# A new issue table for a hand-scheduled kernel: the last token tile computed last in two column halves, and new time constants for the search

## The chip, the cores and the metric

One core of a Trainium2 chip (core 0, the only one that the runs list). The metric is device time in microseconds (us) of one execution, several executions each. Engines are named as in the profile: PE is TensorE (PEld its weight loads), DVE is VectorE, ACT is ScalarE, POOL is GpSimd, SP is SyncE, whose queue SPq issues transfers. The mean granted clock of a run differs (0.989 to 1.000).

## The reference

Two branches read the same layer-normalised input and are added to it. Shapes: 2048 tokens, width 640, hidden width 1728, all bf16.

```python
x = A_q                                   # [1, 2048, 640]
xn = layernorm(x)
# branch A: shifted keys times values, a causal convolution of length 2048 per channel, gated
kv = shift_conv4(k, shift_k) * v
y  = irfft(rfft(pad(kv)) * rfft(pad(ssm_k)))[:2048] + kv * ssm_D
# branch B: gated feed-forward
h  = sigmoid(xn @ w_gate) * (xn @ w_up)   # [2048, 1728]
return x + xn * y + h @ w_down
```

## The kernel before

The sum of all 2048 tokens stays on the chip, and almost everything is bf16. The feed-forward part runs in 4 groups of 512 tokens: 14 hidden chunks of up to 128, each a gate and an up product in PSUM (a "dense group": 5 matmuls of 512 columns), a sigmoid on ACT, a multiply into `hT` on DVE; then for each of the four 128-token tiles of a group a down projection in two column halves of 320. The convolution runs as a four-step Fourier transform in 10 blocks of channels (c1: into `T`, c2: into `S`, products on DVE, c3: into `V`, c4: into `xq`), each step a PE group into one of two PSUM buffers "c", evicted by ACT or DVE.

The instruction stream is not left to a scheduler. All work is recorded as some 950 numbered operations, and two tables, found by an offline search with a cost model, fix the rest: `ORDER` is the order in which they are issued, `ON_DVE` lists those that could run on ACT or DVE and are to run on DVE. The order within each engine is the order in the table; buffers are handed out in that order, too.

```python
ORDER = [6, 0, 5, 1, 4, 2, 8, ...]                    # 948 numbers
ON_DVE = [45, 133, 135, 620, ..., 553, 559]           # 40 numbers

    def table(self):
        dve = set(ON_DVE)
        for i in ORDER:
            o = self.ops[i]
            o.on = next(iter(o.engs)) if len(o.engs) == 1 else "DVE" if i in dve else "ACT"
        return [self.ops[i] for i in ORDER]

    SLOTS = {..., "T": 2, "S": 2, "P2": 1, "V": 1, "c": 2, "g": 4}   # buffers by kind; c and g are PSUM

    def ev(n, out_fn, in_fn, scale=None, **kw):       # an eviction: either engine may do it
        ...
        plan.op({"ACT": ((0.833 * n + 55) * 1e-3, fa), "DVE": ((1.042 * n + 75) * 1e-3, fd)}, **kw)

    def rec_rsq(m0, m1, pri):                         # inverse root of the variances: 13 small DVE instructions
        def rsq():
            nc.vector.tensor_scalar(ve, var, 1.0 / DM, 1e-5, op0=ALU.mult, op1=ALU.add)
            ...                                       # three Newton steps of three instructions
        dve(2400, 1, rsq, r=[("mv", m) for m in range(m0, m1)], ...)   # waits for ACT's sums of squares

    def rec_evac(tr, fc, cs, pri):                    # a pair of dense groups becomes one chunk of hT
        ...
        act(512, lambda: nc.scalar.activation(tl[sg][:], tl[cs[0]][:], ACT.Sigmoid), ...)
        dve(512, 1, lambda: nc.vector.tensor_tensor(hT[:, fc, :], tl[sg][:], tl[cs[1]][:], ALU.mult), ...)

    def rec_down(tr, out):
        for t4 in range(4):
            m = 4 * tr + t4
            last = m == NQ - 1
            parts = ([(0, 7, (0,)), (7, 14, (0,)), (0, 7, (1,)), (7, 14, (1,))] if last else
                     [(c0, c1, (0, 1)) for c0, c1 in ((0, 4), (4, 8), (8, 11), (11, 14))])
            ...
```

The costs in `ev` are constants of the search's model, not measurements: in the trace of the kernel before, an eviction of 1024 columns took 1.02 us on ACT and 1.22 on DVE.

Numbers that come up below: 132 the inverse root for tiles 8 to 15; 649/650 and 653/654 the first two dense pairs of token group 1; 652, 661, 706, 709 multiplies into `hT` for chunks 0, 2, 12, 13 of that group; 163, 164 shift multiplies of the convolution input of block 0; 714 the last part of the down projection of tile 4, which reads `hT` chunks 11 to 13; 227 to 233 second transforms of block 1; 694 a dense group; 180, 232, 258 evictions into `T`, `S`, `T`; 912 to 923 tiles 14 and 15.

Of the kernel before, what the change touches and what calls it, by code (L numbers as in the profile page):

```python
# [22 lines left out]
NQ = S // P  # L23
# [19 lines left out]
def _dft_tables():  # L43
# [37 lines left out]
    6, 0, 5, 1, 4, 2, 8, 7, 3, 11, 10, 13, 12, 9, 14, 16, 71, 72, 15, 73, 74, 75, 91, 17, 86, 76, 96, 77, 104, 97,  # L81
    78, 571, 81, 79, 87, 88, 82, 80, 83, 92, 89, 84, 90, 148, 85, 94, 93, 572, 98, 100, 99, 102, 101, 149, 103, 589,
    42, 150, 151, 152, 155, 153, 57, 154, 157, 563, 156, 158, 564, 64, 565, 590, 567, 566, 568, 569, 62, 573, 570,
    18, 61, 574, 575, 63, 577, 58, 576, 578, 579, 56, 581, 580, 582, 59, 583, 585, 107, 584, 106, 586, 607, 587, 108,
    591, 588, 66, 105, 592, 593, 608, 109, 110, 595, 594, 19, 111, 609, 596, 113, 43, 68, 597, 599, 60, 112, 598, 29,
    600, 601, 114, 603, 65, 604, 605, 602, 610, 67, 606, 611, 612, 39, 614, 613, 44, 615, 45, 133, 134, 20, 136, 616,
    617, 23, 619, 135, 618, 27, 620, 621, 116, 623, 31, 622, 625, 624, 118, 626, 115, 32, 627, 41, 120, 628, 119, 40,
    631, 122, 25, 629, 632, 121, 630, 35, 117, 633, 123, 634, 126, 637, 128, 635, 30, 636, 130, 638, 127, 639, 131,
    26, 640, 129, 37, 643, 642, 125, 641, 649, 124, 650, 132, 24, 651, 38, 653, 644, 655, 652, 21, 654, 162, 22, 69,
    645, 656, 646, 657, 658, 36, 647, 648, 33, 659, 660, 34, 163, 662, 95, 164, 165, 663, 664, 172, 167, 667, 665,  # L90
    137, 28, 661, 159, 666, 669, 166, 668, 161, 168, 47, 671, 160, 670, 50, 169, 672, 673, 48, 171, 143, 170, 46,
    178, 674, 144, 52, 173, 676, 180, 54, 179, 677, 138, 49, 174, 678, 51, 181, 175, 139, 680, 53, 675, 183, 182,
    290, 681, 682, 70, 176, 140, 195, 186, 685, 683, 141, 295, 196, 294, 199, 142, 177, 201, 200, 185, 686, 184, 202,
    145, 197, 293, 187, 689, 296, 198, 679, 291, 188, 687, 690, 292, 203, 297, 204, 192, 692, 189, 694, 205, 193,
    206, 695, 194, 207, 190, 209, 208, 191, 227, 210, 217, 228, 216, 233, 146, 234, 219, 211, 147, 218, 231, 220,
    212, 688, 232, 221, 229, 698, 298, 55, 230, 222, 684, 691, 223, 213, 696, 235, 699, 214, 249, 703, 236, 215, 237,
    701, 224, 238, 248, 704, 226, 240, 251, 225, 243, 239, 250, 259, 244, 697, 735, 260, 253, 265, 736, 693, 707,
    700, 252, 705, 266, 241, 755, 706, 711, 242, 702, 254, 261, 708, 263, 255, 262, 712, 280, 709, 264, 713, 267,
    245, 268, 717, 281, 246, 247, 714, 269, 718, 270, 283, 256, 715, 716, 719, 271, 257, 258, 723, 282, 272, 273,
    310, 274, 710, 720, 311, 275, 722, 721, 314, 276, 729, 315, 316, 299, 286, 312, 317, 730, 288, 313, 731, 318,  # L100
    277, 319, 287, 724, 278, 320, 732, 279, 321, 284, 322, 725, 285, 391, 734, 307, 301, 395, 300, 726, 309, 733,
    756, 737, 333, 308, 302, 324, 727, 739, 728, 394, 342, 323, 325, 738, 304, 397, 343, 303, 396, 344, 740, 346,
    392, 305, 345, 393, 332, 741, 347, 348, 743, 326, 349, 289, 742, 327, 350, 351, 746, 744, 374, 352, 367, 745,
    328, 748, 354, 747, 330, 329, 750, 353, 306, 388, 752, 775, 355, 751, 390, 331, 757, 749, 389, 334, 753, 358,
    336, 759, 356, 335, 359, 398, 754, 758, 337, 357, 338, 761, 760, 400, 368, 763, 401, 762, 399, 403, 369, 404,
    764, 766, 765, 371, 370, 767, 768, 372, 375, 769, 776, 770, 373, 381, 376, 772, 795, 771, 378, 797, 377, 777,
    773, 379, 339, 830, 779, 774, 380, 778, 341, 340, 360, 781, 402, 382, 783, 780, 782, 405, 406, 383, 784, 407,
    786, 384, 433, 385, 432, 411, 788, 785, 787, 435, 412, 386, 417, 436, 415, 418, 387, 790, 416, 413, 792, 789,
    791, 414, 796, 798, 419, 793, 420, 794, 361, 800, 362, 799, 363, 364, 365, 802, 801, 806, 803, 805, 422, 421,
    408, 424, 807, 423, 409, 434, 808, 410, 804, 425, 437, 366, 443, 426, 812, 438, 444, 439, 449, 465, 427, 450,  # L110
    464, 813, 467, 428, 468, 445, 447, 446, 809, 448, 814, 831, 810, 429, 811, 451, 815, 430, 431, 452, 818, 817,
    461, 816, 819, 462, 463, 820, 472, 821, 473, 466, 824, 474, 535, 542, 825, 469, 454, 440, 453, 826, 456, 442,
    827, 455, 441, 470, 459, 822, 457, 471, 460, 823, 549, 832, 829, 458, 556, 828, 475, 834, 499, 476, 833, 500,
    481, 835, 479, 482, 836, 480, 850, 503, 838, 477, 504, 837, 478, 505, 839, 483, 501, 484, 506, 840, 841, 502,
    842, 843, 493, 844, 845, 494, 495, 851, 846, 847, 486, 485, 496, 848, 488, 852, 487, 497, 498, 854, 491, 849,
    489, 492, 853, 490, 507, 508, 517, 855, 856, 518, 521, 858, 523, 522, 870, 857, 510, 871, 524, 509, 519, 859,
    512, 861, 520, 511, 860, 515, 863, 513, 516, 862, 514, 525, 526, 865, 864, 866, 867, 890, 891, 872, 868, 869,
    873, 527, 874, 528, 876, 529, 530, 877, 878, 875, 531, 879, 533, 880, 532, 881, 534, 892, 882, 883, 543, 884,
    885, 544, 887, 886, 545, 546, 893, 888, 550, 547, 895, 894, 889, 548, 551, 896, 897, 552, 553, 900, 554, 898,
    899, 536, 555, 906, 931, 537, 929, 928, 901, 539, 930, 538, 902, 540, 557, 541, 903, 558, 927, 905, 904, 925,  # L120
    907, 560, 559, 924, 908, 561, 926, 909, 562, 910, 912, 911, 934, 918, 932, 935, 919, 933, 920, 922, 942, 921,
    940, 941, 913, 923, 943, 947, 914, 946, 915, 945, 944, 917, 916, 936, 938, 939, 937
]
ON_DVE = [
    45, 133, 135, 620, 622, 34, 144, 179, 183, 141, 196, 145, 146, 266, 247, 258, 315, 329, 773, 340, 416, 364, 448,
    431, 463, 474, 500, 480, 478, 502, 495, 498, 490, 514, 534, 545, 546, 888, 553, 559
# [93 lines left out]
def kernel(  # L220
# [84 lines left out]
    def pe(dur, n, fn, **kw):  # L305
        plan.op({"PE": (dur * 1e-3, fn)}, ni=2 * n, **kw)
# [204 lines left out]
    def rec_st2(idx, pri):  # L511
        T, S_ = f"T{idx}", f"S{idx}"
        tr_ = [(T, x, u) for x in range(2) for u in range(2)]
        for i in range(4):
            c = f"c2_{idx}_{i}"

            def f(i=i, c=c):
                for kk in range(8):
                    k = 8 * i + kk
                    for r in range(2):  # L520
                        for b in range(2):
                            rows = slice(64 * b, 64 * b + 64)
                            nc.tensor.matmul(tl[c][:, b, 64 * kk:64 * kk + 64],  # L523
                                             lhsT=Mb[rows, k, 64 - 64 * r:192 - 64 * r],
                                             rhs=tl[T][rows, 2 * k + r].rearrange("p x j g -> p (x j g)"),
                                             start=(r == 0), stop=(r == 1))
            pe(455, 32, f, r=tr_ + [("Mc",), ("M", i // 2)] + ([(S_, "a")] if i else []), w=[(c,)] + ([] if i else [(S_, "a")]),
               alloc=[(c, "c")] + ([] if i else [(S_, "S")]), pri=CONV + pri, slack=SLK)
            ev(1024, lambda i=i: tl[S_].rearrange("p b x j (g k) -> p b (x j g) k", g=G)[:, :, :, 8 * i:8 * i + 8],
               lambda c=c: tl[c].rearrange("p b (k n) -> p b n k", k=8),  # L530
               r=[(c,)], w=[(S_, i)], pri=pri)
# [33 lines left out]
    def rec_st3(idx, pri):  # L565
        half, sub = divmod(idx, NSUB)
        V, Z, S_ = f"V{half}", f"P{idx}", f"S{idx}"
        for b in range(2):
            c = f"c3_{idx}_{b}"
            zc = idx in PRM["ZC"]  # L570
# [8 lines left out]
            pe(8 * 56.0 * (2 - zc), 8 * (2 - zc), f, r=([(S_, "z", b), (S_, "q", b)] if zc else [(Z, b, 0), (S_, "p", b)]) + [("A",)] + ([] if z else [(V, "a")]),  # L579
# [6 lines left out]
    def rec_st4(half, pri, out):  # L586
        V = f"V{half}"
        vr_ = [(V, s, b) for s in range(NSUB) for b in range(2)]
        for u in range(4):
# [10 lines left out]
            for ih in range(2):  # L600
# [9 lines left out]
                pe(620, 64, f, r=vr_ + [("B",), (xb, u)] + ([(cs[0], "a")] if ih else []), w=[(c,) for c in cs] + ([] if ih else [(cs[0], "a")]),  # L610
# [122 lines left out]
    MG, MD = 215.0, 123.0  # L733
# [37 lines left out]
    def rec_down(tr, out):  # L771
        for t4 in range(4):
# [5 lines left out]
            for c0, c1, ii in parts:  # L778
                def f(c0=c0, c1=c1, t4=t4, pd=pd, ii=ii):
                    for fc in range(c0, c1):  # L780
                        for i in ii:
# [4 lines left out]
                          ([("z",)] if c1 == 14 else []) + ([("cv", u) for u in range(4)] if m >= PRM["ML"] and c0 == 0 else []),  # L786
                          w=[(pd[i],) for i in ii], pri=gt())
# [136 lines left out]
```

## Time and profile before

| | before |
|---|---|
| time, median of 3 (range) | 271.04 us (271.01 to 271.64) |
| span, PE busy, DVE busy, ACT busy | 268.8, 255.5, 189.3, 158.1 us |
| DVE busy from 58 to 122 us | 58.6 of 64 us |
| last matmul, and from there to the end | 263.95, 4.85 us |

How to read the lines: a timeline gives start, length, engine, source line and operation, what is written and read, how many instructions are merged into the line, and in brackets the idle time of the engine before it and what ended it. The timeline of DVE in the kernel before, lines with a wait only:

```profile
57.55 0.17 DVE L662 TENSOR_SCALAR st<-st 128x8 f32<-128x8 f32 x1 [2.24 <-ACT jk L647]
...
64.31 0.41 DVE L317 CAST kt<-c 128x240 bf16<-128x240 f32 x1 [0.43 <-PE c L426]
...
110.20 1.41 DVE L553 TENSOR_TENSOR P<-S 64x1024 bf16<-64x1024 bf16 x2 [0.55 <-ACT S L316]
...
119.17 0.89 DVE L794 TENSOR_TENSOR acc<-g,acc 128x320 bf16<-128x320 f32 x2 [1.62 <-PE g L782]
```

DVE stands 2.24 us for ACT's sums of squares before its inverse root (57.55), and between 64.7 and 110.2 us it never waits by as much as 0.2 us.

### The profile page before, as it was taken

The page shows a single profiled execution, that of the slowest core. Times are in us where ns is not written, and L with a number is a line of the kernel's source. Part 1 is how long each engine was busy: PE and PEld are TensorE (multiplying, and loading weights), DVE is VectorE, ACT ScalarE, POOL GpSimd, SP SyncE. Part 2 cuts the span into 40 slices and gives each one's busy share as a digit, 9 for nine tenths or more (in the row PEclk, how much of TensorE's full clock was granted, in tenths as well). Part 3 has the DMA queues.
Part 4 walks back from the last instruction along what each step waited for, and adds up shares of the span by engine and source line. Part 5 has one row for each costly group of instructions (what it writes and reads, how often), then busy time and mean ns, then how long its engine had stood idle before and what let it go on. Part 6 is the DMA issues. An engine that isn't in the chain of part 4 may idle for free.

```text
span 268.8 us, 9709 instructions
## 1 busy us (share of the span) xinstructions
PE 255.5 (95%) x4375; PEld 155.8 (58%) x4375; DVE 189.3 (70%) x329; ACT 158.1 (59%) x235; POOL 0.7 (0%) x6
## 2 busy tenths in 40 slices
PE   8899998999999697999999999999999999999992
PEld 3754436755455546787656555577676566545771
DVE  5433367257999999866979969698777846558541
ACT  3835939972887696556787456566376666422200
POOL 1000000000000000000000000000000000000000
PEclk9999999999999999999999999999999999999999
DMA  6999999999955191999967072371353647400761
GB/s 181 326 313 263 214 209 154 147 145 296 144 132 127 73 303 32 152 165 148 187 139 208 6 209 67 80 182 40 90 147 123 178 112 214 103 2 5 178 178 40
DMA packets 90448, 40.40 MB, mean 150 GB/s; under 512 B 66592, under 2 KB 88040, under 8 KB 90088
## 3 DMA queue, kind: packets, MB, share of 16 engines
q1 hardware_dynamic: 90216, 39.47, 67.6%
q8 instruction: 34, 0.56, 0.9%
q10 hardware_dynamic: 192, 0.33, 0.3%
q14 instruction: 6, 0.05, 0.1%
HBM read 30.61 MB, written 5.24 MB: 133 GB/s over the span
## 4 chain that ended last, share of the span: by engine, by line
PE 55%; SPq 16%; DVE 14%; DMA 11%; issue 1%; ACT 1%; DVEq 0%
PE g L764 19%; PE g L782 18%; DMA acc<-in_A_q_dram 8%; PE c L523 6%; SPq L445 5%; PE c L607 4%; PE c L575 3%; SPq L423 3%; PE c L577 3%; PE c L503 2%; DVE P L553 2%; DVE ta L473 2%; SPq L353 2%; DMA P<-S 2%; SPq L379 2%; SPq L687 1%
## 5 line engine op out<-in xcount | busy, mean ns | idle before, releaser
L764 PE MATMUL g<-xnT,w 128*128 128x512 bf16 x380 | 89.6, 380 | 0.0
L782 PE MATMUL g<-wd,hT 128*128 128x320 bf16 x448 | 65.4, 299 | 0.0
L764 PEld LDWEIGHTS <-w 128*128 128x128 bf16 x380 | 34.0, 98 | 36.5
L782 PEld LDWEIGHTS <-hT 128*128 128x128 bf16 x448 | 42.1, 98 | 16.9
L730 DVE TENSOR_TENSOR hT<-sig,g 128x512 bf16<-128x512 bf16 x34 | 23.1, 684 | 19.8 <-PE g L764 13.5
L316 ACT CAST S<-c 128x1024 bf16<-128x1024 f32 x31 | 30.8, 1017 | 8.5 <-PE c L523 8.5
L764 PE MATMUL g<-xnT,V 128*128 128x512 bf16 x140 | 31.7, 379 | 0.4 <-ACT sig L728 0.4
L728 ACT ACTIVATE sig<-g 128x512 bf16<-128x512 f32 x34 | 20.2, 595 | 19.6 <-PE g L764 17.0
L523 PEld LDWEIGHTS <-Mt 64*128 64x128 f16 x1280 | 20.4, 95 | 10.2 <-issue 9.5
L523 PE MATMUL c<-T,Mt 64*128 64x64 bf16 x1280 | 23.9, 190 | 1.7 <-ACT V L316 1.6
L794 DVE TENSOR_TENSOR acc<-g,acc 128x320 bf16<-128x320 f32 x32 | 14.3, 484 | 14.9 <-PE g L782 14.9
L316 ACT CAST V<-c 128x1024 bf16<-128x1024 f32 x17 | 17.0, 1014 | 10.7 <-PE c L577 10.7
L764 PEld LDWEIGHTS <-V 128*128 128x128 bf16 x140 | 13.4, 98 | 15.7 <-issue 0.7
L575 PE MATMUL c<-At,S 128*128 128x128 f16 x160 | 19.7, 219 | 2.6 <-DVE S L556 2.2
L722 ACT ACTIVATE sig<-g 128x512 bf16<-128x512 f32 x18 | 10.8, 602 | 16.2 <-PE g L764 16.0
L316 ACT CAST T<-c 128x1024 bf16<-128x1024 f32 x15 | 14.7, 1015 | 9.5 <-PE c L503 9.4
L577 PE MATMUL c<-At,P 128*128 128x128 f16 x160 | 19.6, 219 | 0.0
L575 PEld LDWEIGHTS <-S 128*128 128x128 bf16 x160 | 15.5, 98 | 4.8 <-DVE S L556 4.1
L319 ACT ACTIVATE T<-c 128x1024 bf16<-128x1024 f32 x14 | 13.9, 1024 | 5.6 <-PE c L503 5.6
L553 DVE TENSOR_TENSOR P<-S 64x1024 bf16<-64x1024 bf16 x20 | 13.7, 686 | 4.6 <-ACT S L316 4.2
L577 PEld LDWEIGHTS <-P 128*128 128x128 bf16 x160 | 15.6, 98 | 1.2 <-issue 0.7
L317 DVE CAST S<-c 128x1024 bf16<-128x1024 f32 x9 | 11.0, 1221 | 4.3 <-PE c L523 4.3
(84 smaller groups left out, 265.0 us busy)
## 6 DMA issues: line engine op xcount, KB each, us to landing
w<-in_B_w_gate_dram SPq DMA_DIRECT2D x7, 640.0 KB, 5.0
w<-in_B_w_up_dram SPq DMA_DIRECT2D x7, 640.0 KB, 5.2
kt<-in_A_k_dram SPq DMA_DIRECT2D x8, 320.0 KB, 7.8
vt<-in_A_v_dram SPq DMA_DIRECT2D x8, 320.0 KB, 5.8
xnd<-xq SPq DMA_DIRECT2D x4, 640.0 KB, 5.4
P<-S SPq DMA_DIRECT2D x10, 256.0 KB, 3.8
ht<-in_A_ssm_k_dram SPq DMA_DIRECT2D x16, 96.0 KB, 4.3
wd<-in_B_w_down_dram SPq DMA_DIRECT2D x3, 480.0 KB, 8.8
```

The costliest lines, as they stand in the source:

```text
L316: fa = lambda: nc.scalar.copy(out=out_fn(), in_=in_fn())
L319: fa = lambda: nc.scalar.activation(out_fn(), in_fn(), ACT.Copy, scale=scale)
L445: dma(lambda e, g=g, p=p, c0=c0: e.dma_start(tl[b][g * N1:(g + 1) * N1, :, p, :], h3[:, c0 + j0:c0 + j1, :]), 32 * (j1 - j0), 128, w=[(b, ...
L523: nc.tensor.matmul(tl[c][:, b, 64 * kk:64 * kk + 64], lhsT=Mb[rows, k, 64 - 64 * r:192 - 64 * r], rhs=tl[T][rows, 2 * k + r].rearrange("p ...
L553: dve(n, 2, lambda a=a, o=o, b=b: nc.vector.tensor_tensor(Q(b)[a], X(b)[a], H(b)[o], ALU.mult), r=sr + ([(Z, b, 1)] if h else []), w=[(Z, ...
L575: nc.tensor.matmul(o, lhsT=tl[S_][:, b, 0, j, :], rhs=Ab[:, 2 if zc else 0, :], start=True, stop=zc)
L577: nc.tensor.matmul(o, lhsT=tl[Z][:, b, j, :], rhs=Ab[:, 1, :], start=False, stop=True)
L728: act(512, lambda: nc.scalar.activation(tl[sg][:], tl[cs[0]][:], ACT.Sigmoid), r=[(cs[0],)], w=[(sg,)], alloc=[(sg, "sig")], pri=pri - 2000)
L730: dve(512, 1, lambda: nc.vector.tensor_tensor(hT[:, fc, :], tl[sg][:], tl[cs[1]][:], ALU.mult), r=[(cs[1],), (sg,)], w=[(hk, fc)], pri=pri ...
L764: nc.tensor.matmul(tl[c][:], lhsT=w()[:, k, o:o + P], rhs=tl[X][:, k, :], start=(k == 0), stop=(k == NC - 1))
L782: nc.tensor.matmul(tl[pd[i]][:, 0:320], lhsT=hT[:, fc, t4 * P:(t4 + 1) * P], rhs=wd[:, fc, 320 * i:320 * i + 320], start=(fc == 0), stop=( ...
L794: dve(320, 1, lambda i=i, m=m, pd=pd: nc.vector.tensor_tensor(acc[:, m, 320 * i:320 * i + 320], tl[pd[i]][:, 0:320], acc[:, m, 320 * i:320 ...
```

## The change

Intent: end on a smaller piece of work (tile 15, which already came in two column halves, after tile 14, not before it), and search the table again with other durations for PE's groups (five constants in the diff). The durations steer only the search; they do not enter the program. So the program changes in its tables: the order of nearly all operations after the first 40 us and of some before (there PE's own order stays), and 47 instead of 40 evictions and normalisations on DVE.

```diff
 ORDER = [
-    ... 641, 649, 124, 650, 132, 24, 651, 38, 653, 644, 655, 652, 21, 654, 162, 22, 69, 645, 656, 646, ...
+    ... 641, 27, 132, 644, 21, 24, 33, 649, 38, 650, 651, 162, 34, 653, 652, 69, 163, 654, 655, 164, ...
     (most of the table cut)
-    ... 912, 911, 934, 918, 932, 935, 919, 933, 920, 922, 942, 921, 940, 941, 913, 923, 943, 947, 914, 946, 915, 945,
-    944, 917, 916, 936, 938, 939, 937
+    ... 912, 904, 933, 913, 935, 932, 914, 934, 915, 918, 917, 916, 919, 936, 937, 920, 922, 939, 938, 921, 941, 942,
+    923, 943, 940, 944, 945, 947, 946
 ]
-ON_DVE = [ 40 numbers ]
+ON_DVE = [ 47 numbers; new among those issued between 57 and 122 us: 138, 140, 180, 202, 228, 232, 276, 278, 683;
+           no longer: 179, 196, 247, 266 ]
@@ second transform
-            pe(455, 32, f, ...
+            pe(490, 32, f, ...
@@ third transform
-            pe(8 * 56.0 * (2 - zc), ...
+            pe(8 * 61.5 * (2 - zc), ...
@@ fourth transform
-                pe(620, 64, f, ...
+                pe(660, 64, f, ...
-    MG, MD = 215.0, 123.0
+    MG, MD = 215.2, 136.5
@@ down projection: tile 15 may not start before tile 14 has ended
-                          ([("z",)] if c1 == 14 else []) + ([("cv", u) for u in range(4)] if ...),
-                          w=[(pd[i],) for i in ii], pri=gt())
+                          ([("z",)] if c1 == 14 else []) + ([("cv", u) for u in range(4)] if ...) + ([("last",)] if m == NQ - 1 and c0 == 0 else []),
+                          w=[(pd[i],) for i in ii] + ([("last",)] if m == NQ - 2 and c1 == 14 else []), pri=gt())
```

## The prediction

> **What bounds the kernel now.** I read the page first, then busy time by stretch, the tensor engine's waits, and the timelines of the stretches where it waits. The page:
>
> ```profile
> span 268.8 us, 9709 instructions
> PE 255.5 (95%) x4375; PEld 155.8 (58%) x4375; DVE 189.3 (70%) x329; ACT 158.1 (59%) x235; POOL 0.7 (0%) x6
> ...
> PE   8899998999999697999999999999999999999992
> ```
>
> PE is busy 95% of the span, with its dips in slices 14 and 16 (87 to 94 and 101 to 108 us) and at the two ends. So an order can gain only there. The busy table (us, then PE, PEld, DVE, ACT) shows what stands behind the dips:
>
> ```profile
> 64.00:79.00 15.00, 15.00 (x189) 7.20 (x188) 14.63 (x26) 11.79 (x17) 0.00 (x0) 1.00 0.76 178
> 79.00:105.00 26.00, 22.09 (x483) 13.56 (x482) 25.65 (x45) 19.23 (x23) 0.00 (x0) 1.00 0.53 149
> 105.00:160.00 55.00, 55.00 (x1121) 35.50 (x1120) 45.55 (x72) 35.98 (x46) 0.00 (x0) 1.00 0.79 144
> 264.00:268.80 4.80, 0.00 (x0) 0.00 (x0) 0.86 (x2) 0.00 (x0) 0.00 (x0) 1.00 0.15 38
> ```
>
> From 64 to 105 us DVE is full (40.3 of 41) and PE loses 3.9 us of marked idle; from 105 to 264 us PE is full. The timeline of PE names the waits:
>
> ```profile
> 58.05 1.24 PE L764 MATMUL g<-xnT,V 128*128 128x512 bf16 x5 [0.42 <-ACT sig L728]
> 88.50 0.23 PE L575 MATMUL c<-At,S 128*128 128x128 f16 x1 [0.72 <-DVE S L556]
> 90.67 0.64 PE L523 MATMUL c<-T,Mt 64*128 64x64 bf16 x32 [0.53 <-ACT V L316]
> 93.73 0.64 PE L523 MATMUL c<-T,Mt 64*128 64x64 bf16 x32 [0.53 <-ACT V L316]
> 101.65 0.23 PE L575 MATMUL c<-At,S 128*128 128x128 f16 x1 [1.17 <-DVE S L556]
> 103.81 0.64 PE L523 MATMUL c<-T,Mt 64*128 64x64 bf16 x32 [0.53 <-ACT V L316]
> ```
>
> Two kinds: a third transform (L575) waits for its products on DVE, and transforms in a row wait for one of only two convolution PSUM buffers to be evicted. Ends of matmuls are modelled, so I also took starts: each PE group's start to the next group's start, against the lower quartile of its kind. Excess between 79 and 105 us sums to 5.5 us; after 105 us to some 1.5 us. The tail:
>
> ```profile
> 261.78 4.82 SPq L625 DMA_DIRECT2D out_dram<-acc  x8
> 263.98 0.89 DVE L794 TENSOR_TENSOR acc<-g,acc 128x320 bf16<-128x320 f32 x2 [2.22 <-PE g L782]
> ```
>
> Tile 14 is last: both its column halves accumulate together, so after the last matmul (263.95) come two additions (0.89), then four stores of 40 KB issued until 266.60, then their landing until 268.8: 4.85 us.
>
> [...] DVE-bound 64 to 105 us, PE-bound after. [...] DVE stood still 2.24 us before 57.55 for ACT's statistics, with runnable work behind. [...] the trace has 1.22 (T, S, V casts on DVE) and 1.02 (ACT), so moving an eviction to DVE adds some 1.14 us of DVE pitch (start to start) and frees 1.0 on ACT.
>
> **The change, part by part.** No matmul, eviction, addition or byte is added or removed; the time constants in the diff fed the search and do not enter the program. What changes is the issue table, and evictions or normalisations carried by DVE go from 40 to 47.
>
> 1. Tail. Tile 14 now runs before tile 15, whose two halves are accumulated one after the other. After the last matmul stands one addition (0.49 instead of 0.89), and the last four stores are 20 KB (median landing 1.5 against 1.6 us). But the sync queue issues a store every 0.43 us: four for tile 14, four for the first half and four for the second need 12 x 0.43 = 5.2 us, starting 0.95 after tile 14's last matmul, so they end 6.2 us after it; tile 15 takes 28 x 0.137 = 3.8. Last issue then 2.4 us after the last matmul against 2.65 now. Estimate: -0.3 us with the landing.
>
> 2. Switches on PE. A dense group before a transform costs some 0.1 us more (1.175 against 1.079 before L503; down groups 1.18 against 1.087), a transform after another less (0.476 against 0.57). Counting every pair of neighbours in both tables at these times gives 254.9 us before and 255.3 after (last group aside; it adds another 0.1): +0.5 us.
>
> 3. Convolution PSUM turns, 79 to 105 us. I took each "group, eviction, next group in that buffer" and the PE work between. Seven turns had 0.5 to 1.2 us of work for a 1.2 us eviction in the old table in this stretch; the new one has two, at 1.0 to 1.1. The groups c3, c2, c2, c3, c2, c2 that stood in a row at 88.5 to 94.3 are now parted by three dense groups. If nothing else bound: -3 us.
>
> 4. A new wait near 60 us. The first pair of tile group 1 (650, 653, 654 in the table) used to have a down part between its members, and its fourth product took the buffer of the third. Now two dense buffers alone are in rotation, as the down projection of tile 3 keeps the other two until its last two parts, which moved behind ten dense groups. The fourth product now needs the buffer that the first multiply into hT (L730) frees. That multiply sits on DVE behind the 13-instruction inverse root (57.55 to 60.14), which waits for ACT's statistics, and the new table adds a shift multiply (0.73 with its gap) and the kt copy (0.44) ahead of it. ACT has the same statistics as before, some 0.4 us later since both its tile copies come first: root from 58.0, multiply from 61.7, done 62.3. PE would be ready for the fourth product at 55.30 + 1.09 + 0.10 + 3 x 1.08 = 59.7. New stall about 2.5 us, less the 0.6 us stall at 58.05 that a down part now fills.
>
> 5. DVE chain from 58 to 112 us. It is in order and nearly full, so I added its pitches (0.60 a bf16 operation, 0.72 a product half, 1.14 a PSUM eviction, 0.34 to 0.52 small ones). Before: 60.14 to the end of the first S product at 88.44 with 1.65 us of holes. After: 2.4 us of convolution input work moves behind that product and 1.06 of other work ahead, and the holes close; the product ends at 86.4. PE reaches its third transform at about 86.1 in the new table, with two dense groups (2.2 us) less done, so PE's progress there equals the old one: the stall of step 4 eats the gain of step 3 so far. From there to 105 us the third transforms still wait (about 0.4, 0.2 and 1.0 us), leaving PE about 1.1 us ahead. But the last multiplies into hT for tile group 1 have moved behind more convolution work: the pitches put multiply 12 at 111.0 to 111.6, while the last down part of tile 4, which reads it, now stands at about 110 on PE (before: 12 was done at 107.3 and PE asked at 112.0). Stall 1.6 us, and a wait of 0.4 for an eviction of T on DVE at 116.6. At 118 us PE is then some 0.9 us behind the old table; step 2 is mostly paid there.
>
> 6. After 118 us PE is the bound in both. The margin between second transform and products for blocks 5 and 6 shrinks (9.2 to 8.2 and 12.4 to 9.2 us of PE work), against about 8 that eviction, swap transfer and four products took (168.96 to 177.36 for block 5, less 0.6 as the order of products is now better). Block 9 gains 1.1 us of margin, which should remove its 0.5 us wait at 233. Net 0 +- 0.7.
>
> Sum: +0.9 (at 118 us) +0.1 (rest of step 2) -0.3 (tail) +0 = +0.7, or 271.7. I shade it by 0.5: steps 4 and 5 are sums with 40 terms, and the table was searched for being faster. Prediction **271.2 us**.
>
> **Rivals.** (a) The search is right: the turns of step 3 are the gain, step 4's stall is absorbed since DVE was the bound anyway, and hT arrives in time. For it: turns drop from seven to two, and DVE's holes at 60 to 64 us go. Then -2 to -3 us: 268.5. Against it: DVE has more to do before 112 us, not less. (b) DVE becomes the bound for longer: seven more evictions are 8 us of DVE against 79 us free over the span, but in the stretch that is full each one pushes hT and the products back. Then steps 4 and 5 hold in full and blocks 5 and 6 stall too: 272.5 to 273. (c) Only the tail counts, everything before hidden: 270.7. I hold (a) at a quarter, (b) at a quarter, the rest between. None reaches 2% (5.4 us): all PE excess after 79 us is 7 us, and to be faster by 2% nearly all would have to go; to be slower by 2% a transfer or buffer would have to stop PE anew for 5 us. Range for 8 in 10: **269.0 to 273.0**. Faster 0.03, same 0.95, slower 0.02.
>
> **What would show it.** PE's timeline after: a wait of about 2 us near 60 to 62 us on L730 (step 4); few or no 0.53 us waits on "ACT V L316" (step 3); a wait of over 1 us of a down group (L782) near 110 us on a multiply into hT (step 5); DVE full from 60 to 115 us; one addition of 0.49 last and about 4.5 us from last matmul to end (step 1). PE's last matmul at about 264.9 would fit; at 262 step 5 is wrong, and then most likely because ACT's statistics ended earlier than I place them or hT was not needed when I say.

## The result, and the profile after

| | before | after |
|---|---|---|
| median (range), same rounds, 4 runs each | 271.02 (270.96 to 271.64) | 270.88 us (270.58 to 271.35) |
| span | 268.8 | 269.0 us |
| PE idle beyond the usual from 79 to 105 us | 5.5 | 1.7 us |
| DVE busy from 58 to 122 us | 58.6 | 60.9 of 64 us |
| last matmul, and from there to the end | 263.95, 4.85 | 264.38, 4.62 us |

The ratio is 0.9991, 95% interval 0.9971 to 1.0012: the same. A ratio here is the mean time of one kernel's runs over the mean of the other's runs of the same rounds, so not quite the ratio of the medians. A later set of six runs on another chip gave 1.0059 (see the experiments).

"PE idle beyond the usual" is worked out as in the prediction: from the start of each PE group to the start of the next (starts from the weight loads), less the lower quartile of that kind of pair. Starts are needed here, since 42 records of dense matmuls are missing in the trace after (4333 of 4375). The repeat of this kernel (below), whose records are complete, gives 1.9 instead of 1.7 us. The page after:

```profile
span 269.0 us, 9667 instructions
PE 251.5 (94%) x4333; PEld 155.5 (58%) x4375; DVE 191.6 (71%) x336; ACT 155.8 (58%) x228; POOL 0.7 (0%) x6
...
PE   8999998988999999799999999999999999999993
```

The dips of PE have moved: slices 14 and 16 (87 to 94 and 101 to 108 us) are 9s now, and slices 9 and 10 (53.8 to 67.2 us) and 17 (107.6 to 114.3) are lower. The busy table after, same columns as in the prediction:

```profile
64.00:79.00 15.00, 14.68 (x248) 8.12 (x252) 14.41 (x26) 10.46 (x15) 0.00 (x0) 1.00 0.67 117
79.00:105.00 26.00, 24.19 (x474) 14.80 (x479) 25.59 (x43) 18.40 (x24) 0.00 (x0) 1.00 0.46 131
105.00:160.00 55.00, 51.97 (x1056) 33.35 (x1063) 49.45 (x78) 32.10 (x40) 0.00 (x0) 1.00 0.87 153
```

PE has 2.1 us more in 79 to 105 us than before, and 3.0 less in 105 to 160 (part of that are missing records). DVE is as full as before up to 105 us and 3.9 us fuller behind. Where PE waits now, from its timeline:

```profile
61.74 2.32 PE L765 MATMUL g<-xnT,V 128*128 128x512 bf16 x10 [2.27 <-DVE hT L731]
...
86.07 0.23 PE L576 MATMUL c<-At,S 128*128 128x128 f16 x1 [0.41 <-DVE S L557]
...
101.01 0.23 PE L576 MATMUL c<-At,S 128*128 128x128 f16 x1 [0.71 <-DVE S L557]
...
111.15 1.80 PE L783 MATMUL g<-wd,hT 128*128 128x320 bf16 x12 [1.56 <-DVE hT L731]
...
116.05 0.41 PE L504 MATMUL c<-Ft,ht 32*128 32x64 f16 x30 [0.34 <-DVE T L318]
```

The three waits of 0.53 us on "ACT V" of before are gone. Every wait left above 0.3 us in this stretch is on DVE. (Lines are one higher than before: L765 was L764.) And DVE itself:

```profile
57.55 0.17 DVE L663 TENSOR_SCALAR st<-st 128x8 f32<-128x8 f32 x1 [2.67 <-ACT jk L648]
...
61.01 0.68 DVE L731 TENSOR_TENSOR hT<-sig,g 128x512 bf16<-128x512 bf16 x1
...
68.20 1.23 DVE L321 TENSOR_SCALAR T<-c 128x1024 bf16<-128x1024 f32 x1 [0.49 <-PE c L504]
...
110.41 0.69 DVE L731 TENSOR_TENSOR hT<-sig,g 128x512 bf16<-128x512 bf16 x1
...
122.21 1.23 DVE L318 CAST S<-c 128x1024 bf16<-128x1024 f32 x1 [1.59 <-PE c L524]
```

Between the root at 57.55 and 122.21 us, DVE waits once by more than 0.15 us, for 0.49. The multiply at 61.01 ends the first wait of PE, the one at 110.41 (multiply 12) the fourth. The tail:

```profile
262.52 0.49 DVE L795 TENSOR_TENSOR acc<-g,acc 128x320 bf16<-128x320 f32 x1 [1.01 <-PE g L783]
...
264.42 0.49 DVE L795 TENSOR_TENSOR acc<-g,acc 128x320 bf16<-128x320 f32 x1 [1.41 <-PE g L783]
```

One addition of 0.49 us behind the last matmul instead of 0.89 us for two.

My theory at this point: the parted transforms free PE by some 3.6 to 3.8 us at 79 to 105 us, but DVE's row of work from the root on sets when PE can pass 110 us, and it is no shorter than before. The stall at 61.7 us, the waits at 86 and 101 us and the 1.56 us at 111 are places where that bound shows, not separate costs. Rivals: stalls of PE count one for one, so that removing the 2.3 us at 61.7 gives 2.3 us; or all before the tail is hidden and only the tail counts.

### The profile page after: what moved, and what is told of

Read it like the earlier page. It is cut to its first block, busy times and chain, and to the rows that moved or that the text cites. A ratio compares the mean times of both kernels' runs of the same rounds, so it can differ in the third digit from the quotient of the medians.

```text
span 269.0 us, 9667 instructions
## 1 busy us (share of the span) xinstructions
PE 251.5 (94%) x4333; PEld 155.5 (58%) x4375; DVE 191.6 (71%) x336; ACT 155.8 (58%) x228; POOL 0.7 (0%) x6
## 4 chain that ended last, share of the span: by engine, by line
PE 70%; DVE 16%; ACT 8%; issue 4%; DVEq 0%; ACTq 0%
PE g L765 35%; PE g L783 14%; PE c L524 6%; DVE P L554 4%; PE c L608 4%; ACT jk L648 3%; DVE ta L474 3%; ACT jk L642 2%; PE c L504 2%; PE c L576 2%; PE c L578 2%; PE g L813 2%; DVE tb L469 1%; PE g L745 1%; DVE hT L731 1%
## 5 line engine op out<-in xcount | busy, mean ns | idle before, releaser
L765 PE MATMUL g<-xnT,w 128*128 128x512 bf16 x345 | 84.5, 380 | 3.7 <-issue 2.5
L765 PEld LDWEIGHTS <-w 128*128 128x128 bf16 x380 | 34.1, 98 | 37.2
L317 ACT CAST S<-c 128x1024 bf16<-128x1024 f32 x33 | 33.1, 1021 | 10.7 <-PE c L524 10.7
L765 PE MATMUL g<-xnT,V 128*128 128x512 bf16 x133 | 31.2, 379 | 2.7 <-DVE hT L731 2.3
L317 ACT CAST V<-c 128x1024 bf16<-128x1024 f32 x19 | 18.9, 1019 | 8.6 <-PE c L578 8.6
L765 PEld LDWEIGHTS <-V 128*128 128x128 bf16 x140 | 13.3, 98 | 17.4 <-issue 2.6
L320 ACT ACTIVATE T<-c 128x1024 bf16<-128x1024 f32 x15 | 14.8, 1023 | 8.2 <-PE c L504 8.0
L474 DVE TENSOR_TENSOR ta<-ta,tb 128x1024 bf16<-128x1024 bf16 x20 | 13.8, 688 | 0.2
```

Of the source, the lines that this page charges most:

```text
L317: fa = lambda: nc.scalar.copy(out=out_fn(), in_=in_fn())
L320: fa = lambda: nc.scalar.activation(out_fn(), in_fn(), ACT.Copy, scale=scale)
L474: dve(1024, 2, lambda: nc.vector.tensor_tensor(tl[a][:], tl[a][:], tl[c][:] if c != o else tl[c].rearrange("p b n j -> p n b j"), ALU.add) ...
L765: nc.tensor.matmul(tl[c][:], lhsT=w()[:, k, o:o + P], rhs=tl[X][:, k, :], start=(k == 0), stop=(k == NC - 1))
```

## The experiments

All start from the changed kernel but one (the tail alone), move a few numbers in its tables, and gave correct results. 12 kernels in four sets, each set on a chip of its own, six executions each (five of one version), eleven of the kernel before in every set. Times on these chips spread by 1 to 3 us, more than in the first comparison, so each is read in two ways: the ratio, and the stretch in the trace from one fixed PE group (653, the first group of the second dense pair, just before the first stall) to three later ones. That stretch leaves out what happened before 58 us. Only one of these chips also ran the changed kernel again; where a ratio of another chip is held against its 1.0059, the stretch carries the reading and not the ratio.

| kernel | median us | ratio, 95% interval | 653 to 714 (tile 4's last down part starts) | 653 to 737 (first dense group of token group 2) | 653 to last matmul |
|---|---|---|---|---|---|
| changed kernel, first run | 270.88 | 0.9991, 0.9971 to 1.0012 | 50.92 | 71.71 | 206.15 |
| changed kernel, again | 272.32 | 1.0059, 1.0030 to 1.0088 | 50.90 | 71.69 | 206.92 |
| root behind the multiply | 271.81 | 1.0052, 1.0014 to 1.0090 | 50.89 | 71.67 | 206.37 |
| work in the stall | 271.02 | 1.0025, 0.9997 to 1.0052 | 50.76 | 71.55 | 207.04 |
| hole filled | 269.64 | 0.9957, 0.9929 to 0.9985 | 49.04 | 69.82 | 205.21 |
| multiplies early | 272.44 | 1.0059, 1.0029 to 1.0090 | 51.09 | 72.00 | 206.82 |
| one row | 272.38 | 1.0057, 1.0016 to 1.0097 | 52.64* | 73.42* | 208.62* |
| three off DVE | 270.23 | 0.9993, 0.9961 to 1.0025 | 50.21 | 70.55 | 206.06 |
| three off DVE, late | 272.98 | 1.0071, 1.0050 to 1.0092 | 52.55* | 73.34* | 208.53* |
| hole and three | 268.52 | 0.9913, 0.9898 to 0.9928 | 48.36 | 68.70 | 203.93 |
| all three | 266.71 | 0.9856, 0.9836 to 0.9877 | 48.36 | 67.54 | 202.25 |
| one row on all three | 268.24 | 0.9892, 0.9860 to 0.9925 | 49.05 | 67.71 | 202.50 |

\* In these two profiled runs the granted clock fell to a half for 3.4 us behind the stall; that adds some 1.7 us (see below).

### The changed kernel again

> The changed kernel itself once more, on the chip of the next two runs, as the earlier runs fell on other chips than it did, where times spread more and the granted clock dipped. My theory: 0.997 to 1.003 of before, as the first time; the single runs may spread by 2 us or more where the clock dips to a half for some 3 us after PE has stood still at 61 us, as it did in two of six profiled kernels that keep that stall. Rival: on such a chip the changed kernel is slower than before by 0.3% or more, and the stall is why.

Measured: 1.0059 with an interval clear of 1, so the expected range (up to 1.003) was missed, and the rival's number came true. In the trace the same waits stand at the same distances (50.90 and 71.69 against 50.92 and 71.71). So the table's own behaviour up to 737 repeats to 0.02 us, and the difference between the chips lies elsewhere (the profiled run, 271.05 us, is the second fastest of its six, and so cannot show what the others lost): in the 134.4 us behind 737 (here 135.2, with a wait of 0.64 us of block 5's third transform for its products), and in the clock. What the clock does, from the profile of the kernel with three late evictions moved; the columns are us, PE, PEld, DVE, ACT, POOL, granted clock, DMA share, GB/s:

```profile
60.00:62.00 2.00, 0.17 (x1) 0.10 (x1) 1.97 (x6) 0.23 (x1) 0.00 (x0) 0.96 1.26 237
62.00:65.00 3.00, 3.00 (x8) 1.03 (x7) 2.54 (x6) 0.58 (x1) 0.00 (x0) 0.50 1.10 341
```

PE stood still for 2.24 us, and then got half its clock (0.50) for 3.4 us, so 8 matmuls in 3 us; the ten dense matmuls behind the stall took 3.98 us, against 2.32 in the first run of the changed kernel, with a clock of 1.00. The same followed a stall of 2.42 us in the profile of one row (ten in 3.36 us); in the other five profiled kernels with a stall of over 2 us the clock did not fall there. The mean clock of a run tells such dips (3.4 us at half are 0.006 of 270). Of the 40 executions of kernels with a stall of over 2 us at 61 to 64 us (the changed kernel's first four and 36 on the noisier chips), 15 had a mean clock under 0.9945; of the 29 executions of kernels in which that stall is filled or gone, none. The kernel before had 7 of 44, and ran at 271.67 in those against 270.69 us in the others; the tail alone, with the same first part, had two of six. So a long stall is not the only occasion: in the profile of the tail alone the clock falls to a half at 43.02 us, for 3.41 us, after waits of PE of only 1.27 and 0.47 us. Within the changed kernel and its variants, though, a low clock came only with the stall. Why it falls in some executions and not in others, the runs do not show. So the stall came with a lottery (15 of 40) that cost a run up to 1.7 us, and that is part of why the changed kernel is slower on the noisier chips. It is not all: four of its six runs there had no dip and a mean of 271.60. That rest stays open.

### The root behind the multiply

```diff
-    641, 27, 132, 644, 21, 24, 33, 649, 38, 650, 651, 162, 34, 653, 652, 69,
+    641, 27, 644, 21, 24, 33, 649, 38, 650, 651, 162, 34, 653, 652, 132, 69,
```

> The changed kernel with one entry moved: the 13-instruction inverse root on DVE goes behind the first multiply into hT of tile group 1, instead of ahead of it. My theory (the 2.4 us stall of PE at 61.7 us comes from that order, but what it costs is set later, by DVE's chain, which makes multiply 12 late for the last down part of tile 4): PE's stall near 60 us falls from about 2.4 to under 0.5 us, DVE's chain is at most 0.5 us earlier, the wait of the down part at 109 us grows from 1.7 to 3 us or more, and the whole is 0.2 to 0.6 us faster than the changed kernel (about 270.4 us, 0.998 of before). Rival one (the stall counts in full): 2.4 us faster, about 268.5 us, 0.991 of before. Rival two (nothing before the tail counts): no change, 270.9 us.

Measured: the stall at 61.7 is gone and stands one group later. Timelines of PE and of DVE:

```profile
64.42 0.61 PE L504 MATMUL c<-Ft,ht 32*128 32x64 f16 x32 [2.13 <-DVE ht L450]
```

```profile
59.16 0.69 DVE L731 TENSOR_TENSOR hT<-sig,g 128x512 bf16<-128x512 bf16 x1 [1.82 <-PE g L765]
```

The multiply now goes first but has to wait 1.82 us for its product on PE, and the 2.6 us of root push the convolution input work instead, for which PE's first transform waits 2.13 us. From 653 to 714 it takes 50.89 us, as with the changed kernel (50.92), and the wait at 111 us is still 1.56. My own 0.2 to 0.6 us were not there: I had not seen that DVE would have nothing to do while it waits for PE. Rival one is not decided by this run, since PE stands still for nearly as long as before, at another place; the next run decides it.

### Work in the stall

```diff
-    653, 652, 69, ... 181, 665, 645, 183, 182, 646, 666,
+    653, 645, 646, 652, 69, ... 181, 665, 183, 182, 666,
```

> The changed kernel with two entries moved on PE alone: the last two down parts of tile 3 (1.64 us of PE) stand in the stall of PE near 59 us instead of some 8 us later. DVE's order and load are untouched. My theory (DVE's chain sets the time): the wait near 60 us falls from 2.4 to 0.8 us and PE reaches the evictions at 68 us up to 1.6 us earlier, but DVE's chain can only win the 0.49 us that it waited for PE there, so the waits at 84 and 109 us stay or grow; 0.1 to 0.6 us faster than the changed kernel of the same rounds. Rival (PE's stall counts in full): 1.6 us faster.

Measured: PE does 1.64 us of useful work in the stall, and stands still at 71 us instead:

```profile
62.67 2.32 PE L765 MATMUL g<-xnT,V 128*128 128x512 bf16 x10 [0.74 <-DVE hT L731]
...
71.34 0.69 PE L504 MATMUL c<-Ft,kvt 32*128 32x64 f16 x32 [1.14 <-DVE kvt L485]
```

653 to 714 is 50.76, 0.16 less than with the changed kernel, where the rival (the stall counts in full) had 1.6. PE's time was not what was short. In time it is 0.3% better than the changed kernel on the same chip (1.0025 against 1.0059), with intervals that overlap; none of its six runs had the low clock, against two of six.

### The hole filled

```diff
-    27, 132, 644, 21, 24, 33, 649, 38, 650, 651, 162, 34, 653, 652, 69, 163, 654, 655, 164, 172, 658, 36, 656, 28, 165, 159,
-    657, 660, 167, 659, 160, 166, 137, 662, 161, 661,
+    27, 644, 21, 24, 33, 649, 38, 650, 651, 162, 34, 653, 163, 164, 652, 28, 132, 69, 654, 655, 172, 658, 36, 656, 165, 159,
+    657, 660, 167, 659, 160, 661, 166, 137, 662, 161,
```

> The changed kernel with five entries moved on DVE: two shift multiplies of the convolution input stand ahead of the wait for ACT's sums of squares, where DVE stood still for 2.67 us; the first multiply into hT and one addition stand ahead of the inverse root; the multiply of the next pair stands one place earlier. Nothing is added or removed. My theory (DVE's chain from 58 to 111 us sets the time at 111 us): DVE's idle time before 57.6 us is used, its chain from 64 us on runs 1.6 to 2.2 us earlier, both the stall at 61.7 and the wait at 109 shrink, and the whole is 1.4 to 2.2 us faster than the changed kernel (about 269.0 us, 0.993 of before). Rival one (only PE's stalls count, one for one, the first alone goes): 2.4 us faster, and the same as the run in which the root alone is moved. Rival two (nothing before the tail counts): no change, 270.9 us.

Measured: the 2.67 us in which DVE waited for ACT's sums are used for the shift multiplies, and only 1.1 us of waits (0.61 and 0.49) are left in DVE up to 120 us:

```profile
56.44 0.41 DVE L318 CAST kt<-c 128x240 bf16<-128x240 f32 x1 [0.61 <-PE c L427]
...
58.66 0.69 DVE L731 TENSOR_TENSOR hT<-sig,g 128x512 bf16<-128x512 bf16 x1 [0.49 <-PE g L765]
...
120.49 1.23 DVE L318 CAST S<-c 128x1024 bf16<-128x1024 f32 x1 [1.59 <-PE c L524]
```

653 to 714 falls by 1.9 us, as my theory had it, and the wait at 110 us is the 1.74 us of the ledger unchanged: both sides of it moved. Of the 1.9 us, 0.9 are left at the last matmul; a pause of 0.72 us at 156 us, for which the profile shows no reason, took most of the rest. The ratio is 0.9957 against an expected 0.993, in its interval.

### The multiplies early

```diff
-    702, 710, 265, 253, 708, 712, 252, 266, 709, 713, 254, 267, 245, 706, 246,
+    702, 706, 710, 265, 253, 708, 709, 712, 252, 266, 713, 254, 267, 245, 246,
```

> The changed kernel with two entries moved on DVE: multiplies 12 and 13 into hT stand 3 and 2 of DVE's operations earlier, ahead of evictions and products of the convolution. The stall near 61 us is untouched. My theory: the wait of the last down part of tile 4 (1.7 us at 109) falls to 0.5 us or less, but the evictions passed over come 0.6 to 1.2 us later and some wait of a transform at 105 to 117 us grows; net 0.6 to 1.3 us faster than the changed kernel (about 269.9 us, 0.996 of before). Rival one (DVE's total work up to 117 us is the bound whatever its order): within 0.3 us of the changed kernel. Rival two (the wait counts in full): 1.7 us faster, about 269.2 us.

Measured: the wait of the down part at 111 us is gone, and the wait for `T` grew from 0.34 to 2.07 us:

```profile
115.93 0.41 PE L504 MATMUL c<-Ft,ht 32*128 32x64 f16 x30 [2.07 <-DVE T L318]
```

That is rival one, to the letter: within 0.3 us of the changed kernel (72.00 against 71.71 at 737; 1.0059 against 1.0059). Up to 117 us DVE's sum counts, not its order.

### One row

```diff
-    231, 234, 189, 694, 232, 211, 146, 218, 147, 229, 212,
+    231, 234, 189, 232, 211, 146, 218, 147, 229, 694, 212,
```

> The changed kernel with one entry moved: the dense group that parts three transforms near 93 us goes behind them, so that two turns of the convolution PSUM buffers are tight again as before. My theory (what PE loses between 79 and 105 us is paid out of the wait for multiply 12 at 109 us): PE loses about 1.2 us near 93 us, the wait at 109 us shrinks by about as much, and the whole is 0 to 0.4 us slower than the changed kernel (about 271.0 us, 1.000 of before). Rival (each PSUM turn on PE counts in full): 1.2 us slower, about 272.1 us, 1.004 of before.

Measured: PE loses 0.83 us at the turn, here as a wait on an eviction of `S`, and the wait for multiply 12 stays at 1.56:

```profile
92.01 0.22 PE L576 MATMUL c<-At,S 128*128 128x128 f16 x1 [0.77 <-ACT S L317]
...
112.41 1.80 PE L783 MATMUL g<-wd,hT 128*128 128x320 bf16 x12 [1.56 <-DVE hT L731]
```

The profiled run has the halved clock (0.50) at 63 to 66 us, so its absolute times are late. From the dense group ahead of the row (689) to 714 it takes 24.73 us, and 24.73 in the changed kernel: the lost 0.83 us had vanished before 110 us, because the wait at 99 us had fallen from 0.91 to nothing. (That the wait at 111 would shrink was wrong; the one before it did.) The ratio, 1.0057, is that of the changed kernel on such chips. So parting this one turn was worth nothing to the changed kernel at 714, though it did what it should at its place.

### Three evictions off DVE

```diff
 ON_DVE = [
-    ..., 180, ..., 232, ..., 258, ...
+    (without these three)
```

180 and 232 are among those that the new table gave to DVE; 258 was there before.

> The changed kernel with its table as it is, but three evictions that DVE carries between 72 and 116 us given to ACT, at places where ACT stands idle (T0 second quarter at 72.6, S1 third quarter at 90.4, T3 second quarter at 114.8). My theory (from 58 to 118 us DVE's in-order chain sets the time, and the stalls of PE are only where it shows): each eviction shortens the chain by 1.14 us; the waits of PE at 84, 99, 109 and 115 us (0.59, 0.91, 1.74, 0.53) shrink by two to three us together, and the whole is 2.0 to 2.8 us faster than the changed kernel (0.990 to 0.992 of before), although every order on PE and every count of instructions is the same and PE's stall near 61 us stays. Rival one (the waits on PE come from the order of the table, not from DVE's load): within 0.5 us of the changed kernel. Rival two (ACT becomes the bound or its late evictions block PSUM turns): slower by 0.5 us or more.

Measured: 1.2 us at 737 (70.55 against 71.71), not 2 to 2.8. DVE lost 3.4 us of work and gained waits:

```profile
75.05 0.42 DVE L725 TENSOR_TENSOR hT<-sig,hT 128x512 bf16<-128x512 bf16 x1 [0.65 <-ACT hT L316]
...
77.85 1.22 DVE L317 CAST S<-c 128x1024 bf16<-128x1024 f32 x1 [0.45 <-PE c L523]
...
93.57 1.41 DVE L553 TENSOR_TENSOR P<-S 64x1024 bf16<-64x1024 bf16 x2 [0.48 <-ACT S L316]
...
117.78 1.22 DVE L317 CAST V<-c 128x1024 bf16<-128x1024 f32 x1 [0.87 <-PE c L577]
```

2.45 us of waits, two of them for ACT, which now comes later with what DVE needs. The direction was right, the size was not: the 3.4 us taken off a full in-order engine were worth 1.2, since others were late for what follows. After 737 the gain was lost again in part: at 178 us PE waits 0.70 us for block 5's products, which wait 1.65 us for the swap transfer. The time is 0.9993; the changed kernel had 1.0059, on another chip.

### Three other evictions off DVE, after 122 us

```diff
 ON_DVE = [
-    ..., 315, ..., 389, ..., 341, ...
+    (without these three)
```

> Control. The changed kernel with three other evictions given from DVE to ACT, all after PE has become the bound (S3 third quarter at 122.2, T6 at 149.0, T5 second quarter at 160.8). As much is taken off DVE over the span as in the run with the three early ones. My theory: nothing changes, within 0.4 us of the changed kernel (0.998 to 1.001 of before). Rival (DVE's total load over the span counts, or ACT's slower answers cost): faster or slower by 1 us or more.

Measured: no gain. From the first transform after the stall and the clock dip (at 65.75 us) to the group of the fourth transform at 156.64 us it takes 90.89 us, against 90.92 in the changed kernel; to the last matmul 201.13 against 200.39, of which 0.41 is a pause without a visible reason at 159.6. As much off DVE as in the last run, for nothing: DVE's load counted only where it was full (1.2 us at 737 in the last run, none here). The ratio 1.0071 is outside my number, since that was written for a changed kernel at 0.9991; against 1.0059 it is the same.

### The tail alone

The kernel before, with the last 29 entries of its table in the order of the changed one (but for the four stores of tiles 12 and 13):

```diff
-    912, 911, 934, 918, 932, 935, 919, 933, 920, 922, 942, 921, 940, 941, 913, 923, 943, 947, 914, 946, 915, 945, 944, 917, ...
+    912, 911, 934, 913, 932, 935, 914, 933, 915, 918, 917, 916, 919, 936, 937, 920, 922, 939, 938, 921, 941, 942, 923, 943, ...
```

> The kernel before with only the last 29 entries of its table put in the order of the changed one (tile 14 ahead, tile 15 in two column halves one after the other); everything up to some 259 us is as before. My theory: one addition of 0.49 us instead of two after the last matmul, and from last matmul to end 4.6 instead of 4.85 us: 0.1 to 0.4 us faster than before (0.9985 to 0.9996). Rival one (the tail is what the change is worth, and the rest hides): more than 0.5 us. Rival two (the sync queue's issues of 0.43 us each set the end): no gain or slower.

Measured: 1.0004, interval 0.9980 to 1.0028, which cannot tell 0.1% from nothing. The profile can: last matmul at 265.52 (late from a clock dip to 0.50 at 43 to 47 us), end at 270.1, so 4.58 us instead of 4.85. The last addition:

```profile
265.56 0.49 DVE L794 TENSOR_TENSOR acc<-g,acc 128x320 bf16<-128x320 f32 x1 [1.41 <-PE g L782]
```

The tail is worth 0.27 us by its profile; it could not be shown in the time.

### Hole and three

The edits of "hole filled" and "three off DVE" together.

> The run with DVE's hole before 57.6 us filled, and the three evictions given to ACT as well. My theory: both shorten the same chain, so their gains add until PE itself is the bound: PE has 4.5 us of waits left between 64 and 118 us with the hole filled, of which 2.3 to 3.4 go; some 3.5 to 4.5 us faster than the changed kernel in the stretch up to 118 us, and 3 to 4.5 at the end (0.983 to 0.988 of before, about 266.7 us), if blocks 5 and 6 do not stall in return. Rival (after 118 us transfers and buffers give it back): the gain at 118 us is there, but less than 2 us of it at the end.

Measured: the gains add, 3.0 us at 737 (1.9 + 1.2), and 2.2 at the last matmul. That is short of the expected 3.5 to 4.5, since the evictions bring only the 1.2 us that they brought alone, and 0.9913 is 0.3 points short of what I wrote; it still beats both kernels.

### All three

The same with the two multiplies moved up as well, which alone gave nothing.

> The hole filled, three evictions given to ACT (as in the run that beat both kernels), and multiplies 12 and 13 into hT moved up as well, which alone changed nothing since the eviction behind them then came late. That eviction is now on ACT. My theory: the wait of the last down part of tile 4 (still 1.7 us in the run with hole and evictions) falls to 0.6 or less and little of it comes back at 113 us; 0.8 to 1.7 us faster than that run (0.985 to 0.988 of before, some 267.3 us). Rival (DVE's chain is the bound in any order): within 0.3 us of that run, 0.991 of before.

Measured: another 1.2 us at 737 and 1.7 at the last matmul, 0.9856 of before, the fastest of all. What did nothing alone now pays, since the eviction of `T` that came late behind the multiplies is on ACT. The page:

```profile
PE 255.3 (96%) x4375; PEld 155.5 (59%) x4375; DVE 188.2 (71%) x333; ACT 158.2 (60%) x231; POOL 0.7 (0%) x6
...
PE   8899998999999999999999999999999999999993
```

No dip of PE is left between slice 7 (40 to 46 us) and the last. The ledger of PE's waits after 40 us went from 9.5 us in the repeat of the changed kernel, on the same chip, to 4.9 us, on the same work.

### One row on all three

> The fastest version so far (hole filled, three evictions on ACT, multiplies 12 and 13 earlier), with the edit of the one-row run on top: the dense group that parts three transforms near 90 us goes behind them. In the changed kernel this cost PE 0.83 us there and nothing at 110 us, since the wait for multiply 12 on DVE took it up. Now that wait is gone. My theory: PE again loses 0.7 to 0.9 us at the turn, and this time keeps it: 0.5 to 0.9 us slower than the version without this edit (0.9875 to 0.989 of before, some 267.4 us). Rival (DVE's chain still sets the time at 110 us): within 0.3 us of that version, 0.9856 of before.

The edit of "one row" on the fastest version. Measured: PE loses 0.83 us at the turn again:

```profile
89.14 0.22 PE L575 MATMUL c<-At,S 128*128 128x128 f16 x1 [0.77 <-ACT S L316]
```

and this time 0.69 of it is still there at 714 (49.05 against 48.36), where in the changed kernel nothing was. But at 737 only 0.17 is left, since the fastest version itself waits for DVE again at 113 to 115 us, and 0.25 at the last matmul. So both theories hold in part: up to 113 us PE is now the bound, beyond it DVE is again for a moment. The ratios (0.9892 against 0.9856) come from different chips and do not settle how much of it is this edit.

## Why the prediction was right

The time was right (271.2 predicted, 270.88 measured; PE's last matmul 264.9 predicted, 264.38 measured), and most of its mechanism. A range of 4 us around no change was no hard test; the places and sizes of the waits were. By its steps:

1. **Tail, -0.3.** Right: one addition of 0.49 us, and -0.23 us from last matmul to end (4.85 to 4.62); with the tail alone -0.27. The sync queue took a little longer than written: its last 12 stores run without a break from 261.53 to 266.95 us, 5.4 instead of 5.2, and the last ends 2.57 us behind the last matmul instead of 2.4.
2. **Switches, +0.5.** Right. Counted with start to start times from complete records (the kernel before and the repeat of the changed one, lower quartiles of each kind of pair over both), a dense group took 1.175 us before a first transform and 1.079 before another dense group, and PE's work at its usual pace grows by 0.41 us, and by 0.54 with the last group (seven matmuls, 0.95 us, instead of six, 0.82).
3. **PSUM turns, -3 if nothing else bound.** Right: the excess from 79 to 105 us fell by 3.8 us (3.6 by the complete records of the repeat). The clause "if nothing else bound" carried the prediction; "one row" shows a turn costing 0.83 us at its place and nothing at 714.
4. **A new wait near 60 us, 2.5 us.** It came as placed, 2.43 us (the timeline shows 2.27), though I had the root at 58.0 and it began at 57.55, and PE was ready 0.4 us sooner than I had it. What I made of it was wrong, however. I wrote that "the stall of step 4 eats the gain of step 3 so far". When the stall was moved on (root behind) or filled with work (work in the stall), PE reached 714 within 0.2 us of the same time. The stall eats nothing; DVE's row does, and the stall is where PE first runs into it.
5. **DVE's chain.** Right, and here it was close: third transform at 86.1, measured 86.07; multiply 12 ending at 111.0 to 111.6, measured 111.09; the down part's stall 1.6, measured 1.56 in the timeline (1.74 by starts); a wait of 0.4 for `T` at 116.6, measured 0.34 at 116.05. "Multiplies early" and "hole filled" show that this sum, not the order, sets the time at 117 us. One reading was too wide: from 64 to 79 us PE was full as well (15.00 of 15), so its 3.9 us of idle all lie in 79 to 105.
6. **After 118 us, net 0 +- 0.7.** Block 9's wait went (0.5 us at 233 before, none after). Blocks 5 and 6 kept their margin in the first run; in the repeat block 5 cost 0.64 us, and in faster versions the swap transfer of block 5 took 0.2 to 0.9 us back. From 737 to the last matmul it was 134.46 us before and 134.44 after (the same groups, in another order), 135.23 in the repeat.

Rival (a), the search is right and the stalls are absorbed, fell: PE's stalls are absorbed, but into DVE's bound, so no gain came of it. Rival (b), DVE the bound for longer, had the mechanism (steps 4 and 5 came nearly in full) but not the size: blocks 5 and 6 did not stall in the first run, and the seven more operations on DVE added 2.3 us to its busy time (189.3 to 191.6), not 8. Rival (c), the tail alone, gives nearly the right number for the wrong reason: the 3.8 us less between 79 and 105 us were real, but over all PE's waits after 40 us sum to 8.4 us before and 9.5 in the repeat (0.6 of it at block 5), and the switches come on top.

The shade of 0.5 us that I took off the sum of 271.7 was a guess without a working; the sum itself would have been 0.8 us high. A gain of about that size stands in the traces where the prediction did not look, in the first 43 us. PE does the same groups in the same order there, but waits less for the normalised tiles of token group 1. Before, then after:

```profile
41.04 0.73 PE L700 MATMUL g<-ident,xq 128*128 128x128 bf16 x10 [1.27 <-DVE xq L678]
42.24 0.73 PE L700 MATMUL g<-ident,xq 128*128 128x128 bf16 x10 [0.47 <-DVE xq L678]
```

```profile
40.07 0.45 PE L701 MATMUL g<-ident,xq 128*128 128x128 bf16 x5 [0.54 <-DVE xq L679]
40.88 0.45 PE L701 MATMUL g<-ident,xq 128*128 128x128 bf16 x5 [0.36 <-ACT xq L681]
41.70 0.76 PE L701 MATMUL g<-ident,xq 128*128 128x128 bf16 x10 [0.36 <-ACT xq L681]
```

The first down projection starts at 42.29 instead of 42.81 us; 0.28 of these 0.52 us stand in every profile of the changed kernel and its variants, the rest lies within the scatter of the start. From there to 737, with the same groups in between, PE takes 0.96 us more than before, and the prediction had 0.9 at 118 us. So from there on its sum was nearly exact, and the guess happened to cover a gain that it had not seen: that part was luck.

And the range did not know of chips where this table is 0.6% slower than before (272.32, inside the range of 269.0 to 273.0).

## What to carry to other kernels

When one engine is full for a long stretch and issues in order, add up its row of work before judging another engine's waits: a wait that was moved or filled here changed next to nothing (0.03 and 0.16 us at 714), since that row neither started sooner nor got shorter. To shorten it, first use the time in which the full engine itself waits (1.9 us here), then take work off it (1.2 us here, for 3.4 us less work), and check who will now be late for the work behind. An edit that alone does nothing (multiplies early) can pay (1.2 us at 737) once the neighbour that took back its gain has been moved, so try such edits again after each step: three small edits of a searched table gave 1.4%, where the search had given nothing. Add start to start times, not durations: bf16 operations of 0.69 us start 0.60 us apart here (61.61 and 62.21 us in the profile after), so a sum of durations is some 15% too long.
